# An attention kernel on one core: TensorE's order taken from a written list, some products split into column tiles, the eps sums on another engine

## The chip, the cores and the metric

The kernel runs on one core of a Trainium2 chip. The core has TensorE (PE in the profile; PEld is its weight load), VectorE (DVE), ScalarE (ACT), GpSimd (POOL) and SyncE (SP), which issues nearly all DMAs here. The metric is the device time of one execution in microseconds. Three runs of the kernel before gave 334.11, 334.47 and 336.25 us; the median, 334.47, is the time to beat.

## The reference

Two independent attention layers over 2,048 tokens of width 640, with 32 heads of 20; their outputs stand side by side.

```python
# A: four segments of 512 tokens, with a memory M, z carried from one to the next
for s in range(N):
    qs, ks, vs = (q[:, :, s].copy(), k[:, :, s].copy(), v[:, :, s].copy())
    logits = jnp.einsum('bhqd,bhkd->bhqk', qs, ks) * scale + mask      # causal within the segment
    p = _softmax(logits, axis=-1)
    a_dot = jnp.einsum('bhqk,bhkd->bhqd', p, vs)
    pq = phi(qs)                                                       # t + 1 if t > 0 else exp(t)
    num = jnp.einsum('bhld,bhde->bhle', pq, M)
    den = jnp.einsum('bhld,bhd->bhl', pq, z)[..., None] + 1e-06
    a_mem = num / den
    o = g * a_mem + (1.0 - g) * a_dot
    outs.append(o)
    pk = phi(ks)
    M = M + jnp.einsum('bhld,bhle->bhde', pk, vs)
    z = z + jnp.einsum('bhld->bhd', pk)
return o @ wo
# B: the same projections from one wqkv; scores of a window of 256 tokens, softmax, p @ v, @ wo
```

## The kernel before, in words

The work is cut into eight chunks of 512 tokens, numbered n = 0 to 7: A and B take turns (even n is A, odd n is B). For each chunk TensorE makes the projections q and k (five pieces of 128 columns, each five products of 512 columns; `qk_job`), v (two halves of four tiles, each five products of 320 columns; `v_job`), the scores, the value sums, for A from the second segment on the memory products (`mem`) and the update of the memory (`dm_job`), and at last the output products (`final_job`, `last_job`). All whole-array products pass through `wide` (L870).

Scores come in 153 batches (`score_batch`, L758). A batch fills two of three score buffers in PSUM; ScalarE takes the exponential of each (L774), GpSimd cuts the triangles (L813) or VectorE multiplies the small end squares (L791). A batch can start only when ScalarE has emptied the first buffer of the batch before. What TensorE does between two batches I call a visit: visit i lies between batch i-1 and batch i, counted from 0. When all batches of a group of four heads are done, the value sum of that group follows (`av`, L827; for the last chunk `av_tile`, L848): four column tiles of 32 work side by side, one head each. VectorE turns the result (L883) and takes the reciprocal of the denominators (L908), GpSimd multiplies (L918). For a memory product of an A chunk, VectorE first adds eps to the denominators (L903) and then takes the reciprocal (L906); GpSimd multiplies into a buffer u and VectorE adds it to the output (L931).

All other results of TensorE go through two PSUM banks, m0 and m1, which VectorE empties: q and k (L501), v (L677, L682), outputs (L1027).

The array has three modes here: whole (128 rows by 128 columns), four row tiles of 20 rows for scores, four column tiles of 32 columns for value sums.

The o of a finished chunk is stored to DRAM by SyncE (L949) and read back transposed (L968, DMA_TRANSPOSE) as the weights of the output products. The transposed tile of chunk n takes a buffer that chunk n-2 used, so its transpose is issued after the last output product of chunk n-2. The last chunk is stored and transposed in four tiles; the fourth is turned on TensorE instead (L1049, L1061).

The order of the instructions on every engine is fixed when the program is built, by a planner. Class `Flow` keeps a clock for each engine with costs written in the code; `body` walks its loop: a score batch if its buffer is free, otherwise a value sum or memory product whose inputs are there by those clocks (one queue, `pend`), otherwise a step of the first job in the list that can go. Evictions and small vector work are put on their engines by `at`, `when_idle` and `blocked` by the same clocks. `room` holds back batches of small squares and value sums when TensorE got more than 160 matmuls within 3 us. On the chip each engine follows its own list in order and waits on semaphores.

## Time and profile before

| | |
|---|---|
| median of three runs | 334.47 us |
| the profiled execution | 334.4 us |
| its span, first to last instruction | 331.6 us |
| granted clock of TensorE | 1.000 |
| TensorE busy | 315.6 us (95%), 6583 matmuls recorded |
| ScalarE busy | 302.4 us (91%) |
| VectorE busy | 264.2 us (80%) |
| GpSimd busy | 256.3 us (77%) |
| DMA | 47.36 MB, mean 143 GB/s |
| first exponential starts, last ends | 9.1 us, 318.3 us |

Busy times are unions of what the profiler recorded; matmuls and exponentials overlap with their successors, so the distance from one start to the next tells more than a duration. Times in timelines are microseconds from the first instruction; a row is start, length, engine, line, operation, tiles, shape and count, and in brackets the idle time ahead of it with what ended it. "Issue" is a wait that no semaphore of the profile explains. A few per cent of the matmul records are missing.

### The profile page before, as it was taken

How to read it: one execution, taken by the hardware profiler on the slowest of the kernel's cores; microseconds unless marked ns; L12 is line 12 of the kernel's file. 1: busy time of each engine (PE TensorE's matmuls, PEld its weight loads, DVE VectorE, ACT ScalarE, POOL GpSimd, SP SyncE). 2: the span in 40 equal slices, each digit the busy share in tenths (PEclk: the TensorE clock that was granted, in tenths of full speed). 3: DMA queues.
4: the chain of work that ended last, by engine and by line, in shares of the span. 5: the costliest groups of instructions: out<-in, count | busy, mean ns of one | idle time of the engine just before them, and what ended most of it. 6: DMA issues, size and time to landing. Idle time of an engine off the chain costs nothing.

```text
span 331.6 us, 15794 instructions
## 1 busy us (share of the span) xinstructions
PE 315.6 (95%) x6583; PEld 174.4 (53%) x6619; DVE 264.2 (80%) x556; ACT 302.4 (91%) x333; POOL 256.3 (77%) x648
## 2 busy tenths in 40 slices
PE   8999999999999999989999999999999999999896
PEld 3444546455444455546644545455654545666564
DVE  6777767798978899989868898888667889876654
ACT  1979999999999999999999999989999999999841
POOL 8366689998659799975867879996875969977750
DMA  6975746566596852335699145044555154769852
GB/s 198 396 253 152 173 135 125 136 175 176 132 226 132 165 155 63 67 86 122 183 208 181 42 94 156 3 104 80 148 140 114 21 150 122 166 142 187 178 127 100
DMA packets 76260, 47.36 MB, mean 143 GB/s; under 512 B 48381, under 2 KB 73181, under 8 KB 76189
## 3 DMA queue, kind: packets, MB, share of 16 engines
q1 hardware_dynamic: 75469, 45.71, 56.7%
q8 instruction: 51, 0.84, 1.1%
q10 hardware_dynamic: 720, 0.66, 0.7%
q14 instruction: 20, 0.16, 0.2%
HBM read 17.62 MB, written 16.96 MB: 104 GB/s over the span
## 4 chain that ended last, share of the span: by engine, by line
PE 57%; DVE 15%; ACT 10%; issue 7%; POOL 6%; DMA 3%; SPq 1%; ACTq 0%; DVEq 0%; POOLq 0%
PE m L870 36%; PE sc L758 11%; ACT pt L774 10%; PE m L827 6%; POOL pt L813 4%; DVE pt L791 4%; PE m L848 2%; DVE tt L883 2%; POOL u L918 2%; DVE pq L542 2%; DVE kA L501 2%; DVE vA L677 1%; DMA xT<-in_A_x_dram 1%; DVE pq L536 1%; DVE ot L1027 1%
## 5 line engine op out<-in xcount | busy, mean ns | idle before, releaser
L774 ACT ACTIVATE pt<-sc 128x1024 bf16<-128x1024 f32 (+2 forms) x306 | 285.0, 1012 | 10.7 <-PE sc L758 8.6
L813 POOL TENSOR_SCALAR_AFFINE_SELECT pt<-pt 128x128 bf16<-128x128 bf16 (+1 forms) x512 | 177.1, 374 | 60.4 <-ACT pt L774 57.4
L883 DVE STREAM_TRANSPOSE tt<-m 128x512 f32<-128x512 f32 x88 | 61.4, 711 | 20.0 <-PE m L827 9.1
L918 POOL TENSOR_TENSOR o<-tt,rr 128x320 bf16<-128x320 f32 x64 | 47.8, 747 | 4.1 <-DVE rr L908 4.0
L870 PEld LDWEIGHTS <-xT 128*128 128x128 bf16 x350 | 32.0, 97 | 24.2 <-issue 12.3
L758 PE MATMUL sc<-qB,kB 20*64 20x64 bf16 (+2 forms) x1728 | 38.6, 218 | 1.4 <-issue 0.8
L791 DVE TENSOR_TENSOR pt<-pt,ends 128x1024 bf16<-128x1024 bf16 (+2 forms) x50 | 36.3, 740 | 0.0
L758 PEld LDWEIGHTS <-kB 20*64 20x64 bf16 (+1 forms) x1728 | 21.7, 98 | 23.3 <-issue 22.0
L758 PE MATMUL sc<-qA,kA 20*64 20x64 bf16 (+4 forms) x1024 | 33.1, 237 | 0.5
L1027 DVE CAST ot<-m 128x320 bf16<-128x320 f32 x56 | 26.9, 485 | 7.4 <-PE m L870 7.1
L870 PEld LDWEIGHTS <-oT 128*128 128x128 bf16 x280 | 24.7, 98 | 11.4 <-issue 1.1
L870 PE MATMUL m<-wBv,xT 128*128 128x320 bf16 x160 | 27.0, 299 | 2.4 <-DVE tt L883 2.3
L870 PE MATMUL m<-wv_A,xT 128*128 128x320 bf16 x160 | 26.0, 299 | 2.0 <-DVE vA L677 1.9
L870 PE MATMUL m<-xT,wBq 128*128 128x512 bf16 x96 | 26.4, 381 | 0.4 <-issue 0.2
L870 PE MATMUL m<-xT,wq_A 128*128 128x512 bf16 x88 | 25.0, 381 | 1.8 <-DVE vA L677 0.8
L870 PE MATMUL m<-xT,wk_A 128*128 128x512 bf16 x96 | 25.6, 388 | 1.1 <-DVE qA L501 0.7
L870 PE MATMUL m<-xT,wBk 128*128 128x512 bf16 x84 | 24.8, 381 | 0.8
L758 PEld LDWEIGHTS <-kA 20*128 20x128 bf16 (+1 forms) x1024 | 13.5, 97 | 20.6 <-issue 19.6
L827 PE MATMUL m<-pt,vA 128*32 128x192 bf16 (+3 forms) x512 | 23.6, 275 | 0.0
L870 PE MATMUL m<-wo_A,oT 128*128 128x320 bf16 x140 | 22.7, 300 | 0.2
L501 DVE CAST kB<-m 128x512 bf16<-128x512 f32 x20 | 13.8, 691 | 9.4 <-PE m L870 9.4
L870 PE MATMUL m<-wo_B,oT 128*128 128x320 bf16 x120 | 19.4, 300 | 0.3 <-DVE ot L1027 0.3
(112 smaller groups left out, 405.3 us busy)
## 6 DMA issues: line engine op xcount, KB each, us to landing
out_dram<-ot SPq DMA_DIRECT2D x29, 160.0 KB
scr_o<-o SPq DMA_DIRECT2D x28, 160.0 KB
xT<-in_B_x_dram SPq DMA_DIRECT2D x8, 288.0 KB
xT<-in_A_x_dram SPq DMA_DIRECT2D x8, 256.0 KB
scr_pk<-e SPq DMA_DIRECT2D x15, 128.0 KB
vS<-vA SPq DMA_DIRECT2D x16, 87.0 KB
vL<-vB SPq DMA_DIRECT2D x8, 174.0 KB
scr_kA<-kA SPq DMA_DIRECT2D x16, 60.0 KB
```

The source lines that it names most:

```text
L501: nc.vector.tensor_copy(out=dst[:, m, at:at + L], in_=ps[:, :])
L542: nc.vector.tensor_tensor(out=r if len(box) == 1 else e, in0=r, in1=e, op=ALU.min)
L758: nc.tensor.matmul(ps[j // 2][h0:h1, j % 2, c0:c0 + nq], lhsT=k[rows, g, k0:k0 + h1 - h0], rhs=q[rows, g, q0:q0 + nq], start=True, stop=Tr ...
L774: nc.scalar.activation(out=pt[:, :, lo:hi], in_=ps[i][:, :, lo:hi], func=ACT.Exp, scale=self.scale)
L791: nc.vector.tensor_tensor(out=blk, in0=blk, in1=self.ends[:, c0, :].unsqueeze(1).unsqueeze(1) .to_broadcast([P, 2, n // SH, SH]), op=ALU.mult)
L813: nc.gpsimd.affine_select(out=blk, in_=blk, pattern=pat, compare_op=ALU.is_ge, fill=self.zero, base=base, channel_multiplier=mul)
L827: nc.tensor.matmul(O[HD * j:HD * j + HD, q0:q0 + nq], lhsT=v[:, at_head(h):at_head(h) + HD], rhs=pts[j // 2][:, j % 2, c0:c0 + nq], start= ...
L848: nc.tensor.matmul(O[HD * j:HD * j + HD, o0:o0 + nq], lhsT=v[:, at_head(h):at_head(h) + HD], rhs=pts[j // 2][:, j % 2, c0:c0 + nq], start= ...
L870: self.nc.tensor.matmul(ps[:, 0:n], lhsT=lhsT, rhs=rhs, start=start, stop=stop)
L883: self.nc.vector.transpose(out=tt[:], in_=O[:, :])
L918: nc.gpsimd.tensor_tensor(out=to[:] if add_to else to, in0=a, in1=b, op=ALU.mult)
L1027: nc.vector.tensor_copy(out=ot[:, 320 * hf:320 * hf + 320], in_=ps[:, 0:320])
```

## The change

TensorE's order is now a written list, `PLAN`. An entry is a unit and a count: S or s is the next score batch, A the next value sum, M the next memory product, and a letter with chunk and piece one product (k, q, v, o), one piece of the memory update (d) or one step of the end (z0). `k70*7` is seven products of k of chunk 7. The loop only takes what stands first in the list; the planner's clocks say when, and still place everything on the other engines. Memory products have a queue of their own, `memq`, and wait in the planner for the group's value sum.

In a visit that starts with a capital S and has a value sum in it, `wide` issues each product as four products of 32 columns each into the four column tiles. There are 42 such visits, the last one visit 117; the list's last part has small s only, or no value sum.

The eps sum goes from VectorE to GpSimd. The planner's model changes: the fetch of instruction blocks takes the place of `room`, VectorE and GpSimd hold each other up on some operations, and several costs are lower. No DMA and no other computation is added or removed.

```diff
@@ -26,11 +26,13 @@
 EPS = 1e-6
 NPT = 10
 AT = 0
-FETCH = 160
-FETCH_NS = 3000
+BLOCK = 256
+BLOCK0 = 170
+BLOCK_NS = 3900.0
 BACK = 800.0
 NTT = 4
 QPOOL = 750.0
+EPS_NS = 170.0
 GAP = 48
 GATE = 9800.0
 NM = 20
@@ -53,6 +55,32 @@
 LANES = 8
 AHEAD = 100.0
 LEAD = 500.0
+HOLD = 1
+SPARE = 150.0
+COL_NS = 3.0
+PLAN = (
+    "k00*5 q00*5 k01*4 S k01 q01*5 S v00*16 S v00*4 k02 S k02*4 k03*5 q02*3 S q02*2 q03*5 k04*5 "
+    "A S A q04*5 v01 s v01*9 s k10*5 S v01*10 S q10*2 A S q10*3 q11*3 S q11*2 q12*5 A s k11*5 "
+    "k12*2 S k12 A k12*2 S v10*9 S v10*10 S v10 A k13*2 s k13*3 q13*4 S q13 A s k14*5 q14*2 S "
+    "q14*2 A q14 S d2*5 v11*4 S v11*8 S v11*3 A v11 S v11*4 d2*2 S q20*4 A s q20*5 s q20*6 "
+    "k20*6 S k20*4 A s k20*5 v20*5 S v20*3 A v20 s v20 q23*5 v20 s v20*8 S v20 q23*5 A s v21*5 "
+    "k23*3 S k23*2 A s o00*5 k23*5 v21*5 S o00*5 v21*5 S A v21*5 s q30*5 k30*2 S k30*3 A s "
+    "k30*6 S k30*4 q30 S q30*4 A s M q30*5 v30*2 s v30*3 A S M v30*10 s A M s v30*5 q33*4 S q33 "
+    "A s M k33*5 q33 s q33*4 k33*3 S k33*2 A s M v31*8 S v31*2 A M S v31*10 S A M S d4*5 q40*3 "
+    "S q40*2 d4*2 A s M k40*5 s q40*10 S v40*5 k40*5 A S k40*5 v40*5 S v40*2 A v40*2 S v40*6 "
+    "q43*3 S q43*7 S k43*10 A S o00*5 A s o10*10 s o00*5 o10*5 S o00*10 v41*4 S v41 o10*5 A "
+    "o00*2 s o00*3 v41*5 S A o00*5 s v41*8 s v41*2 o10*7 S o10*3 A o10*3 s o10*2 q50*5 S A "
+    "k50*3 s k50*2 k53*5 s q50*5 k50*2 s k50*3 A S k50*2 M k50*3 s A M S v50*5 q50*5 s A M S "
+    "v50*10 S v50*5 A s M q53*6 s q53*4 k53*2 S k53*3 A S M v51*9 S v51 A M S v51*10 S A M S "
+    "q60*5 d6*5 s d6*2 A S k60*2 M k60*3 q60*5 s k60*6 S k60*4 q60*5 A S q63*5 v60*5 S A v60*5 "
+    "s q63*5 v60*2 S v60*3 k63*5 S v60*5 A k63 S k63*4 o10*5 S o20*3 A s o20*7 s v61*10 S v61*5 "
+    "A v61*5 S o30*5 o20*5 S o20*5 A o20 S o20*4 o30*4 s o30 o20*10 S A o20*4 S o20 k70*7 S k70 "
+    "A k70*2 S k70*5 v70*3 S v70*2 q70*4 s q70 A s M q70*6 s q70*4 A s k73*5 s v70*5 A s M "
+    "v70*7 s v70*3 A M s q73*2 M q73*3 s k73*5 q73*2 s q73*3 A s M o30*5 s v71*5 A s M o30*5 "
+    "v71 s v71*4 A M s v71*10 s A M s o30*10 s o40*5 o30*5 s o30*5 A s o40*10 s o40*10 A o40*5 "
+    "s o40*5 o50*3 s o50*2 o40*5 o50*2 s o50*3 A s o50*10 s A o50*2 s o50*9 s o50*9 s A o60*5 s "
+    "o60*5 o70*5 A o70 s o70*4 o60*5 s o60*5 o71*4 s o71*6 o60*2 s o60*6 A o60*8 A o60*4 o72*2 "
+    "z0*4 ")
 
 def at_head(h):
     return VS * h + 12 * (h // 16)
@@ -97,23 +127,26 @@
                     self.slow[m] = had < (0.355 if self.slow.get(m - 1, True) else 0.31)
         return not self.slow[k]
 
-    def room(self, n):
 ...
     def on_pe(self, mode, ns, cols, ready=0.0, n=1):
-        self.issued.append((max(self.pe, ready), n))
-        return self.on_pe_(mode, ns, cols, ready)
+        self.count += 1
+        if mode != self.mode:
+            self.pe += 97.0
+            self.mode = mode
+        t = max(self.pe, ready)
+        self.on_pe_(mode, ns, cols, ready)
+        first, self.sent = self.sent, self.sent + 2 * n
+        at = (first - BLOCK0) // BLOCK + 1
+        while BLOCK * at + BLOCK0 <= self.sent:
+            x = t + (self.pe - t) * (BLOCK * at + BLOCK0 - first) / (2.0 * n)
+            wait = self.block - x
+            if wait > 0.0:
+                self.starved += wait
+                self.pe += wait
+                t += wait
+                x += wait
+            self.block = x + BLOCK_NS
+            at += 1
+        return self.pe + 215.0
 
     def on_pe_(self, mode, ns, cols, ready=0.0):
         if mode != self.mode:
@@ -867,8 +923,18 @@
 
     def wide(self, ps, lhsT, rhs, n, start, stop):
 
-        self.nc.tensor.matmul(ps[:, 0:n], lhsT=lhsT, rhs=rhs, start=start, stop=stop)
-        self.f.on_pe("full", mm_ns(n), n)
+        f = self.f
+        if self.by_tiles:
+            for j in range(4):
+                s = slice(HD * j, HD * j + HD)
+                self.nc.tensor.matmul(ps[s, 0:n], lhsT=lhsT[:, s], rhs=rhs, start=start,
+                                      stop=stop, tile_position=(0, HD * j),
+                                      skip_group_check=True)
+            f.on_pe("col", n / 2.4 + COL_NS, n, 0.0, 4)
+        else:
+            self.nc.tensor.matmul(ps[:, 0:n], lhsT=lhsT, rhs=rhs, start=start, stop=stop,
+                                  skip_group_check=True)
+            f.on_pe("full", mm_ns(n), n)
         self.f.left = 0 if stop else self.KT - 1 if start else self.f.left - 1
 
     def turn(self, O, bi):
@@ -898,15 +964,18 @@
             a = a.rearrange("p (g b) d -> p g b d", g=4)
             b = b.rearrange("p (g b) d -> p g b d", g=4)
 
-        def s1():
+        def s0():
+            nc.gpsimd.tensor_single_scalar(out=rr[:], in_=tv[:, :, DH], scalar=EPS, op=ALU.add)
+            t = f.on_pool(EPS_NS, t0)
+            f.when_idle(t, lambda: s1(t))
+
+        def s1(te=None):
             if add_to:
-                nc.vector.tensor_single_scalar(out=rr[:], in_=tv[:, :, DH], scalar=EPS,
-                                               op=ALU.add)
-                f.on_dve(100.0, t0)
                 nc.vector.reciprocal(out=rr[:], in_=rr[:])
+                t1 = f.on_dve(276.0, te)
             else:
                 nc.vector.reciprocal(out=rr[:], in_=tv[:, :, DH])
-            t1 = f.on_dve(276.0, t0)
+                t1 = f.on_dve(276.0, t0)
             f.at(t1 - 100.0, lambda: s2(t1))
 
         def s2(t1):
@@ -929,14 +998,17 @@
                     return
                 self.adds.remove(add)
                 nc.vector.tensor_tensor(out=dst, in0=dst, in1=to[:], op=ALU.add)
-                t3 = f.on_dve(300.0, t2)
+                t3 = f.on_dve(210.0, t2, True)
                 self.done_with(uslot, t3)
                 if last:
                     last(t3)
             self.adds.append(add)
             f.when_idle(t2, add)
 
-        f.when_idle(t0, s1)
+        if add_to:
+            f.at(t0 - 100.0, s0)
+        else:
+            f.when_idle(t0, s1)
 
     def final(self, n, o, scr, wo, out2d, r0, col, t0, t1, t):
 
@@ -1338,11 +1410,26 @@
         started = -1
         i = 0
         late = [(19500.0, self.zero_end), (45000.0, self.consts_e), (60000.0, self.consts_one)]
+        plan = PLAN.split()
+        plan = [x.split("*")[0] for x in plan for _ in range(int((x + "*1").split("*")[1]))]
+        visits, tiles = [False], False
+        for x in plan:
+            if x in "Ss":
+                visits.append(False)
+                tiles = x == "S"
+            elif x == "A" and tiles:
+                visits[-1] = True
+        plan.reverse()
+        over = set()
         while True:
             f.flush()
             times = []
             self.all_scored = i == len(bs)
-            if i < len(bs):
+            while plan and plan[-1] in over:
+                plan.pop()
+            want = plan[-1] if plan else None
+            self.by_tiles = bool(plan) and visits[i]
+            if i < len(bs) and want in (None, "S", "s"):
                 n, ent, ms, complete = bs[i]
                 kind, c = chunks[n]
                 if self.ring("pt", NPT) is not None:
@@ -1351,8 +1438,10 @@
                         for w in "kq":
                             need.append(self.done.get((n, w, e[0])))
                     if None not in need:
-                        t = max(need + [f.room(4 * len(ent)) if ent[0][1][0] in "lust" else 0.0])
-                        if t <= f.pe and not self.may_wait():
+                        t = max(need)
+                        if t <= f.pe and (want or not self.may_wait()):
+                            if want:
+                                plan.pop()
                             if n != started:
                                 started = n
                                 self.seed(n + 1)
@@ -1368,40 +1457,59 @@
                             for g in complete:
                                 pend.append((n, g, "tile" if n == NC - 1 else "av"))
                                 if kind == "A" and c > 0:
-                                    pend.append((n, g, "mem"))
+                                    memq.append((n, g))
                             i += 1
                             if i == len(bs) or bs[i][0] != n:
                                 self.mark(f.seen, n, "scored")
                             continue
                         times.append(t)
             soon = times[-1] if times else None
-            if pend:
+            if pend and want in (None, "A"):
                 n, g, what = pend[0]
                 kind, c = chunks[n]
                 if what == "tile":
                     ps_ = [p for x in range(4) for p in parts[(n, g[1] + x)]
                            if p[1] // P == g[0]]
                     need = [whole(p[6] for p in ps_), self.done.get((n, "v", g[1]))]
-                elif what == "av":
+                else:
                     ps_ = parts[(n, g)]
                     need = [whole(p[6] for p in ps_), self.done.get((n, "v", g))]
-                else:
-                    need = [self.done.get(("dm", c - 1)),
-                            self.done.get((n, "pq", g) if g < KT else (n, "pq2"))]
-                if None not in need and not (f.open and 0 < f.left <= 3):
-                    t = max(need + [min(f.bank_free), f.room(
-                        4 * len(ps_)) if what != "mem" else 0.0])
+                if None not in need and (want or not (f.open and 0 < f.left <= 3)):
+                    t = max(need + [min(f.bank_free)])
                     wait = (f.mode == "full" and soon is not None and len(pend) < 3
                             and soon < f.pe + 2200.0 and self.more(f.pe))
-                    if t <= f.pe and not wait:
+                    if t <= f.pe and (want or not wait):
+                        if want:
+                            plan.pop()
                         pend.pop(0)
                         self.one_group(n, kind, c, g, what, parts, left, o_t, groups_done,
+                                       scro, wo, out2d)
+                        continue
+                    times.append(t)
+            if memq and want in (None, "M"):
+                n, g = memq[0]
+                kind, c = chunks[n]
+                need = [self.done.get(("dm", c - 1)),
+                        self.done.get((n, "pq", g) if g < KT else (n, "pq2")),
+                        self.done.get((n, "add", g))]
+                if None not in need and (want or not (f.open and 0 < f.left <= 3)):
+                    t = max(need[:2] + [min(f.bank_free)])
+                    after = f.pe + mm_ns(L) + (97.0 if f.mode != "full" else 0.0)
+                    wait = (len(memq) < HOLD and max(f.bank_free) > after + SPARE
+                            and self.more(f.pe))
+                    if t <= f.pe and (want or not wait):
+                        if want:
+                            plan.pop()
+                        memq.pop(0)
+                        self.one_group(n, kind, c, g, "mem", parts, left, o_t, groups_done,
                                        scro, wo, out2d)
                         continue
                     times.append(t)
             hit = None
             for x, jb in enumerate(self.jobs + self.fins):
                 if f.open and not jb[0] is self.opener:
+                    continue
+                if want and jb[2] != want and (jb[2][0] != "d" or jb[1] in ("bank", 0.0)):
                     continue
                 t = self.need_time(jb[1])
                 if t is None:
@@ -1420,6 +1529,10 @@
                     jb[1] = next(jb[0])
                 except StopIteration:
                     (self.jobs if jb in self.jobs else self.fins).remove(jb)
+                    over.add(jb[2])
+                if f.count != was:
+                    if want:
+                        plan.pop()
                 while late and f.pe > late[0][0]:
                     late.pop(0)[1]()
                 continue
```

Left out are the changed planner costs (`on_dve`, `on_pool` and their callers), the labels given to jobs, and the mark that the value sum of a group is normalised.

More of the change, by code (lines that the diff above doesn't have):

```diff
@@ L87, in __init__ @@
         self.slow = {}
-        self.issued = []
+        self.sent, self.block, self.starved = 0, 0.0, 0.0
+        self.dve_at, self.pool_at = [], []
+        self.count = 0
     def full_rate(self, t):
@@ L98, in full_rate @@
         return not self.slow[k]
-    def room(self, n):
-        while self.issued and self.issued[0][0] <= self.pe - FETCH_NS:
-            self.issued.pop(0)
-        have = n + sum(k for _, k in self.issued)
-        t = self.pe
-        for t0, k in self.issued:
-            if have <= FETCH:
-                break
-            have -= k
-            t = t0 + FETCH_NS
-        return t
-    def on_pe(self, mode, ns, cols, ready=0.0, n=1):
-        self.issued.append((max(self.pe, ready), n))
-        return self.on_pe_(mode, ns, cols, ready)
+    def on_pe(self, mode, ns, cols, ready=0.0, n=1):
+        self.count += 1
[17 more added lines that the diff above has]
+        return self.pe + 215.0
     def on_pe_(self, mode, ns, cols, ready=0.0):
@@ L137, in on_act, with held, on_dve @@
         return self.act + 181.0
-    def on_dve(self, ns, ready=0.0):
-        self.dve = max(self.dve, ready) + ns
+    def held(self, t, by):
+        for a, b in by:
+            if a <= t < b - 65.0:
+                return b - 65.0
+        return t
+    def on_dve(self, ns, ready=0.0, shared=False):
+        t = max(self.dve, ready)
+        if shared:
+            t = self.held(t, self.pool_at)
+            self.dve_at = self.dve_at[-7:] + [(t, t + ns)]
+            for x, (a, b) in enumerate(self.pool_at):
+                if t < a < t + ns - 65.0:
+                    late = t + ns - 65.0 - a
+                    self.pool_at[x:] = [(p + late, q + late) for p, q in self.pool_at[x:]]
+                    self.pool += late
+                    break
+        self.dve = t + ns
         return self.dve + 138.0
     def on_pool(self, ns, ready=0.0):
-        self.pool = max(self.pool, ready) + ns
+        t = self.held(max(self.pool, ready), self.dve_at)
+        self.pool_at = self.pool_at[-11:] + [(t, t + ns)]
+        self.pool = t + ns
         return self.pool + 98.0
@@ L1163, in batches, with job @@
         return out
-    def job(self, gen):
-        return [gen, next(gen)]
+    def job(self, gen, label):
+        return [gen, next(gen), label]
     def may_wait(self):
@@ L1222, in seed @@
                     need = [tx, gate] + ([self.known("wB" + what, some[0])] if first else [])
-                    add(self.qk_job(n, what, some, w, dst, need, self.scr[what + kind][c], phi))
+                    add(self.qk_job(n, what, some, w, dst, need, self.scr[what + kind][c], phi),
+                        "%s%d%d" % (what, n, some[0]))
                 if first and some[0] == AT:
-                    add(self.late_v())
+                    add(self.late_v(), "v01")
             if first:
                 v[3] = v[3] + [self.known("wBv", half)]
-            add(self.v_job(n, half, *v))
+            add(self.v_job(n, half, *v), "v%d%d" % (n, half))
     def body(self, xA, A_wq, A_wk, A_wv, A_wo, A_beta, xB, B_wqkv, B_wo, out2d):
@@ L1318, in first @@
                                       self.known(0, "x", KT - 1 if m else 0)],
-                                     scr[what + "A"][0], phi)))
+                                     scr[what + "A"][0], phi),
+                         "%s0%d" % (what, m)))
         for m in range(KT):
@@ L1415, in body @@
                 jb = (self.jobs + self.fins)[hit]
+                was = f.count
                 if jb[1] == "bank":
@@ L1438, in body @@
             f.pe = max(f.pe + 1.0, min(times))
-        assert i == len(bs) and not pend and not self.jobs and not self.fins
+        assert i == len(bs) and not pend and not memq and not self.jobs and not self.fins
     def used_pt(self, left, i, g):
```

28 lines of the change are left out of this document (14 added, 14 removed).

## The prediction

> **What bounds the kernel.** I read the page first, then the timeline of TensorE, then the groups with their shapes kept apart, the waits, and the tail in every engine's timeline. The execution that was profiled took 334.4 us, its span 331.6, so 2.8 us lie around the span; the median of the three runs is 334.47, and I work with 334.4. A difference under about 1% (3.3 us) could not be told from no change.
>
> The page's totals, the 40 slices of TensorE and ScalarE, and the instruction queue:
> ```profile
> PE 315.6 (95%) x6583; PEld 174.4 (53%) x6619; DVE 264.2 (80%) x556; ACT 302.4 (91%) x333; POOL 256.3 (77%) x648
> ...
> PE   8999999999999999989999999999999999999896
> ...
> ACT  1979999999999999999999999989999999999841
> ...
> q8 instruction: 51, 0.84, 1.1%
> ```
> Two engines are full from slice 3 to slice 38, in step with each other: a score batch may not start before ScalarE has emptied the buffers of the one before. Busy times overlap with themselves, so I take durations from starts. TensorE's timeline near the end, and a value sum of chunk A:
> ```profile
> 96.60 0.59 PE L827 MATMUL m<-pt,vA 128*32 128x448 bf16 x12
> 97.02 0.29 PE L827 MATMUL m<-pt,vS 128*32 128x64 bf16 x16
> 97.14 0.20 PE L827 MATMUL m<-pt,vA 128*32 128x64 bf16 x4
> ...
> 314.02 0.39 PE L758 MATMUL sc<-qB,kB 20*128 20x128 bf16 x13 [0.84 <-issue]
> 314.35 1.53 PE L870 MATMUL m<-wo_A,oT 128*128 128x320 bf16 x10
> 315.81 0.40 PE L758 MATMUL sc<-qB,kB 20*128 20x128 bf16 x16
> 316.14 0.30 PE L848 MATMUL m<-pt,vB 128*32 128x128 bf16 x8
> ...
> 320.15 2.21 PE L870 MATMUL sc<-wo_A,oT 128*128 128x320 bf16 x15
> 322.20 0.84 PE L870 MATMUL m<-wo_B,xT 128*128 128x320 bf16 x5
> ```
> Fifteen products of 320 columns take 322.20 - 320.15 = 2.05 us, 0.137 each. Ten of them followed by scores take 315.81 - 314.35 = 1.46: ten products (1.36) and 0.10 for the change of mode (whole array, rows in four, columns in four). Counted along the timeline there are 382 changes of mode: 37 us. With 0.137 for 320 columns, 0.216 for 512 (the median distance of two starts), 0.23 for scores of 512 columns, 0.55 for a batch of the small squares and 0.57 to 0.70 for a value sum, TensorE's work is 269 us, with the changes 306. It runs from 0.8 to 328.5, so it stands idle 21 us, 3 of them before the first scores.
>
> ScalarE:
> ```profile
> 314.49 3.77 ACT L774 ACTIVATE pt<-sc 128x1024 bf16<-128x1024 f32 x4 [0.95 <-PE sc L758]
> ```
> Four exponentials in 3.77 us, the last ending 1.03 after its start: 0.913 from start to start. 284 of these, 20 narrower ones at about 0.70 and 18 of phi at 0.95 or 0.55 come to some 288 us, between 9.1 and 318.3: 21 us of slack here too. So neither engine alone is the bound; what counts is how evenly the order spreads TensorE's work over the 153 visits between score batches, and what is left after the last.
>
> **The change, part by part.**
>
> *Changes of mode: -4.3.* Walking the list gives 392 changes if every product used the whole array. In 42 visits the products are split into four column tiles, which takes away 54: 338 remain, 44 fewer than 382, at 0.097. The split costs no array time by the rows above: the twelve matmuls of 448, 320 and 192 columns are three groups of four tiles over 960 columns and take 0.42 us, 0.140 per 320, against 0.137 for a whole product. Weight loads do not show either: 16 matmuls over 64 columns with their 16 loads take 97.14 - 97.02 = 0.12 us, 0.03 for four. The Trainium skill (TensorEngine Tiling (Array Packing), Restrictions and Gotchas) says that column tiling gives up the fast weight load, which speaks against the split. If four loads then stood in line at the 97 ns that the trace gives one, a product of 320 columns would take 0.39 instead of 0.14; the 0.03 above says that they do not.
>
> *Work moved ahead of the last score batch: nothing in the sum of TensorE, +0.6 in balance.* The list leaves 28 output products after the last scores (o60 18, o72 10), where the timeline of before has 60: 32 x 0.137 = 4.4 us leave the tail and enter the visits. The changes of mode saved there just pay for them: visits 1 to 152 hold 287.6 us of TensorE in both orders, ScalarE 287. Taking the larger of the two engines in stretches of eight visits gives 293.1 before, 293.9 after; in stretches of four 295.2 and 297.6, since a few visits of the list are heavy (140: fifteen output products and a value sum, 3.4 us against 1.8 of exponentials). Other visits differ little: 62 of the 64 value sums stand at the same visit. Bounds 0 and +2.4; I take +0.6, nearer to eight, as the exponentials of phi can slide into heavy visits.
>
> *Eps on GpSimd: -2.0.* Groups by shape, then waits (total, times, longest):
> ```profile
> L903 DVE TENSOR_SCALAR rr<-tt 128x16 f32<-128x16 f32 x24 | 8.9, 371 | 0.0
> ...
> L906 DVE RECIPROCAL rr<-rr 128x16 f32<-128x16 f32 x24 | 6.1, 253 | 0.8
> ...
> L651 POOL TENSOR_TENSOR MZ<-mz,bm 128x36 bf16<-128x36 f32 x3 | 1.6, 517 | 0.0
> ...
> PE m L870 <- DVE tt L883: 2.3, 12, 0.2
> ...
> PEld L827 <- DVE rr L906: 2.0, 6, 0.4
> ```
> VectorE loses 24 x 0.37 = 8.9 us, all in the three stages with memory products. The minimum of L903 is 0.15, its median 0.26, its maximum 1.01, so much of this is waiting, not work. What of it reaches TensorE: 2.0 us of value sums that waited for the reciprocal, and the 2.3 us of products behind transposes. Both gone would be -4.3, neither 0; I take the first, -2.0. GpSimd gains 24 sums. The nearest rows are L651 (0.52 mean, 36 elements) and the 0.15 of the cheapest L903: 3.6 to 12 us in stages where it is busy 80% (26.3 of 33.0 us from 91 to 124). I count nothing, because a mask has some two visits until its value sum. Two waits are added: GpSimd's sum waits for VectorE's transpose, with masks and multiplications queued behind it, and VectorE's reciprocal waits for the sum, with evictions behind it. If that cover fails, 24 x 0.1 to 0.2 us reach TensorE, +2.4 to +4.8.
>
> *The tail: +0.7 and +0.8.* SyncE's transposes and a copy of VectorE, from the timeline:
> ```profile
> 306.14 3.90 SPq L968 DMA_TRANSPOSE oT<-scr_o  x1
> ...
> 318.59 1.21 SPq L968 DMA_TRANSPOSE xT<-scr_o  x1
> ...
> 323.54 0.68 DVE L1053 CAST pq<-sc 128x512 bf16<-128x512 f32 x1
> ```
> Before, TensorE never stops after the last scores: output products fill every wait. The list ends with o72 and z0. After z0's first four products the copy (0.68) must be done before the last two halves, and nothing but z0's 16 small matmuls lies beside it: about +0.7, bounds 0 and 1.5. And o72 needs the third transposed tile. Before, the value sum of visit 150 ended near 310.0 and that tile landed at 321.4, used at 322.2: 12.2 us. The list puts the sum in visit 149 and o72 some 10 us of TensorE later. SyncE then waited on other stores, so part of the 12 is queue: +0.8, bounds 0 and 2.8.
>
> *Instruction supply: 0.* Splitting 190 products adds 6 instructions each, 1,140 on 13,202: 56 packets on q8 instead of 51 (259 instructions per packet now). By pure TensorE work, before has 6 stretches of 256 instructions shorter than 3.9 us (the closest packets of q8 start 3.5 to 3.9 us apart), short by 4.8 us together; after has 8, short by 8.3. Most shortfalls vanish since ScalarE holds the pace, which is the cover; the stall of 0.84 at 314.02 is one that showed. Uncovered: +3.5.
>
> *The rest: 0.* Separate queue for memory products, labels, the planner's new costs: they set the order on VectorE, GpSimd and SyncE, no instruction more. The DMAs are the same in number; stores and transposes of the outputs move up by three or four visits on SyncE.
>
> Sum: -4.3 + 0.6 - 2.0 + 0.7 + 0.8 = -4.2: 334.4 - 4.2 = **330.2 us**.
>
> **Rivals.**
>
> *Landings eat the gain: 333.5.* The order is rigid. o30 ends in visit 138 and o50 starts in visit 141: some 7 us, where before o30's end (294.0) to the tile's landing (301.1, after the transpose issued at 296.39) and first safe use took 7.5. The same with o60 after o40 (some 9.5 us against 7.9). Half a microsecond at o50, the full 2.8 at o72 instead of 0.8 and 0.5 elsewhere give +3.0 to +3.3. For it: such waits hide in no other work of a fixed order. Against: two of the three have slack.
>
> *Instruction supply decides, slower: 337.0.* Place: visits 102 to 103, 145 to 146, 64 to 66, 87 to 89, where tiled products, scores and a value sum stand together (200 instructions in one visit against some 125 before). If ScalarE's pace does not cover the shortfalls, the 8.3 us show, of which before already pays about 1.5: +6.8, to 337.0. Five stalls of 0.84 cancel the gain; from there it is slower. Against: the densest visits stand next to thin ones, and packets come ahead of need.
>
> *Split products are dearer: from 341.* If the loads did not hide in part, at 0.06 more for each of 190 products: +11. The value sums' rows speak against it. The loss of the fast weight load in the Trainium skill (same page and section) would be its cause.
>
> **Chances.** Forecast 0.66, own range 325.5 to 333 (0.56 of it below 331.1); landings 0.20; supply 0.11; split products 0.03. Best corner: -4.3 - 4.3 and no waits at the end, 325.8; two of ten left out, the range is 325.5 to 335.5. Faster by over 1% 0.56, within 1% 0.10 + 0.20 + 0.03 = 0.33, slower 0.08 + 0.03 = 0.11.
>
> **What would show it.** Groups of 32-column products on L870's successor in steps of 0.137 and 0.216; some 338 changes of mode; L903 on POOL near 0.2 to 0.5; last scores about 2 to 3 us earlier than 315.8 and a tail of about 13 us instead of 15.8; q8 with 56 packets and no more "issue" gaps on scores. The forecast is wrong if TensorE waits on transposed tiles at o50, o60 or o72, if 0.8 us gaps on "issue" multiply, or if the middle is more even than my stretches say.

## The result, and the profile after

| | before | after |
|---|---|---|
| median | 334.12 us (22 runs) | 332.59 us (22 runs) |
| ratio | | 0.9952, 95% interval 0.9935 to 0.997 |
| profiled execution, its span | 334.4, 331.6 us | 332.5, 330.7 us |
| first scores start | 8.7 | 8.8 |
| first to last scores | 307.1 | 309.1 |
| last scores to the end of the span | 15.8 | 12.8 |

The change gains 1.6 us; I forecast 4.2. The time lies in the range. The ratios here and below leave out runs that took over 1.5% longer than the fastest of their kernel: of the changed kernel's 22 these are two, of 337.6 and 338.1 us. Two later measurements of the same kernel (e9 and e16) gave ratios of 0.9976 (0.9948 to 1.0005) and 0.9969 (0.9939 to 1.0), so 0.8 to 1.6 us is what it is worth.

The page of the changed kernel: totals, the 40 slices of TensorE and ScalarE, and the instruction queue.
```profile
PE 316.4 (96%) x7195; PEld 176.2 (53%) x7195; DVE 255.8 (77%) x533; ACT 299.6 (91%) x333; POOL 265.4 (80%) x672
...
PE   7999999998999999999999999999999999999984
...
ACT  1979999998999998989999999899999999979962
...
q8 instruction: 56, 0.92, 1.2%
```
As before, two engines are full from slice 3 to slice 38, but ScalarE has a dip (7) in slice 36, from 289 to 298 us. The 56 packets are there.

Products split into column tiles, in TensorE's timeline:
```profile
211.94 1.05 PE L930 MATMUL m<-xT,wk_A 128*32 128x512 bf16 x16
212.81 1.25 PE L930 MATMUL m<-xT,wq_A 128*32 128x512 bf16 x20
```
Sixteen matmuls, four products of 512 columns, take 212.81 - 211.94 = 0.87 us: 0.217 each, as a whole product does. The same count of changes of mode as for before gives 338.

The sum of eps on its new engine, and the reciprocal behind it (groups of the page):
```profile
L968 POOL TENSOR_SCALAR rr<-tt 128x16 f32<-128x16 f32 x24 | 7.4, 309 | 2.7 <-DVE tt L949 0.5 <-DVE rr L977 0.3 <-POOL pt L869 0.2
L974 DVE RECIPROCAL rr<-rr 128x16 f32<-128x16 f32 x24 | 5.5, 232 | 0.7 <-POOL rr L968 0.6
```

Who waits for whom (total, times, longest), after, and below it the one row of before that it is to be read against:
```profile
ACT pt L830 <- PE sc L814: 12.9, 23, 1.9
...
PE m L935 <- DVE tt L949: 1.3, 6, 0.3
...
PEld L883 <- DVE rr L974: 1.2, 4, 0.4
```
```profile
ACT pt L774 <- PE sc L758: 8.6, 20, 1.5
```
The two rows that I wanted to shrink did: TensorE behind the transposes 2.3 to 1.3, value sums behind the reciprocal 2.0 to 1.2. But **ScalarE waits for scores 12.9 us instead of 8.6**, and the longest wait is new. It is visit 140, which the list gives fifteen output products and a value sum (L904, not shown) between two score batches:
```profile
290.35 0.40 PE L814 MATMUL sc<-qB,kB 20*128 20x128 bf16 x16
...
290.69 1.53 PE L935 MATMUL m<-wo_A,oT 128*128 128x320 bf16 x10
...
293.01 0.85 PE L935 MATMUL m<-wo_A,oT 128*128 128x320 bf16 x5
...
293.80 0.93 PE L814 MATMUL sc<-qB,kB 20*64 20x64 bf16 x64
...
294.79 4.69 ACT L830 ACTIVATE pt<-sc 128x1024 bf16<-128x1024 f32 x5 [1.95 <-PE sc L814]
```
From scores to scores TensorE needs 293.80 - 290.35 = 3.45 us. ScalarE has two exponentials, 1.83 us, to do in that time, and stands still for 1.95.

The end, TensorE's timeline:
```profile
313.98 0.85 PE L935 MATMUL m<-wo_A,oT 128*128 128x320 bf16 x5
...
315.68 0.72 PE L935 MATMUL m<-wo_B,xT 128*128 128x320 bf16 x4 [0.84 <-DMA xT<-scr_o]
...
317.92 0.40 PE L814 MATMUL sc<-qB,kB 20*128 20x128 bf16 x16
...
324.60 0.30 PE L1133 MATMUL sc<-one,o 128*32 128x32 bf16 x16
...
325.46 0.72 PE L935 MATMUL m<-wk_A,pq 128*128 128x320 bf16 x4 [0.56 <-DVE pq L1125]
```
The last scores start 2.1 us later than before, and the tail behind them is 3.0 us shorter. The products of o71 wait 0.84 us for their transposed tile, those of z0 0.56 for the copy.

### The profile page after: what moved, and what is told of

It reads as the page before. It is cut to its first block, busy times and chain, and to the rows that moved or that the text cites. A ratio compares the mean times of both kernels' runs of the same rounds, so it can differ in the third digit from the quotient of the medians.

```text
span 330.7 us, 16968 instructions
## 1 busy us (share of the span) xinstructions
PE 316.4 (96%) x7195; PEld 176.2 (53%) x7195; DVE 255.8 (77%) x533; ACT 299.6 (91%) x333; POOL 265.4 (80%) x672
## 4 chain that ended last, share of the span: by engine, by line
PE 36%; DVE 5%; ACT 3%; DMA 2%; POOL 2%; issue 1%; SPq 1%; ACTq 0%; DVEq 0%
PE m L935 19%; PE sc L814 7%; PE m L883 5%; ACT pt L830 3%; PE m L930 2%; DVE tt L949 2%; PE m L904 1%; DMA xT<-scr_o 1%; DVE pt L847 1%; DMA scr_o<-o 1%; POOL pt L869 1%; DVE kA L557 1%; POOL o L987 1%; DVE ot L1099 0%; PE m L686 0%
## 5 line engine op out<-in xcount | busy, mean ns | idle before, releaser
L830 ACT ACTIVATE pt<-sc 128x1024 bf16<-128x1024 f32 (+2 forms) x306 | 282.9, 1026 | 15.1 <-PE sc L814 12.9
L949 DVE STREAM_TRANSPOSE tt<-m 128x512 f32<-128x512 f32 x88 | 61.2, 709 | 24.7 <-PE m L883 15.9
L935 PEld LDWEIGHTS <-xT 128*128 128x128 bf16 x296 | 26.7, 97 | 18.4 <-issue 6.1
L935 PEld LDWEIGHTS <-oT 128*128 128x128 bf16 x244 | 21.5, 97 | 12.5 <-issue 3.3
L935 PE MATMUL m<-wBv,xT 128*128 128x320 bf16 x147 | 24.2, 299 | 0.9 <-DVE tt L949 0.4
L935 PE MATMUL m<-xT,wBq 128*128 128x512 bf16 x82 | 21.4, 380 | 0.3 <-DVE tt L949 0.3
L935 PE MATMUL m<-xT,wBk 128*128 128x512 bf16 x81 | 20.7, 381 | 0.0
L935 PE MATMUL m<-wv_A,xT 128*128 128x320 bf16 x119 | 20.0, 300 | 0.2 <-DVE vA L733 0.2
L738 DVE CAST vB<-m 128x320 bf16<-128x320 f32 x32 | 15.6, 488 | 5.4 <-PE m L935 3.1
L557 DVE CAST qB<-m 128x512 bf16<-128x512 f32 x20 | 13.8, 688 | 6.7 <-PE m L930 3.4
L935 PE MATMUL m<-xT,wk_A 128*128 128x512 bf16 x69 | 17.7, 379 | 1.2 <-DMA xT<-in_A_x_dram 1.1
```

Of the source, the lines that this page charges most:

```text
L557: nc.vector.tensor_copy(out=dst[:, m, at:at + L], in_=ps[:, :])
L738: nc.vector.tensor_copy(out=dst, in_=src)
L830: nc.scalar.activation(out=pt[:, :, lo:hi], in_=ps[i][:, :, lo:hi], func=ACT.Exp, scale=self.scale)
L935: self.nc.tensor.matmul(ps[:, 0:n], lhsT=lhsT, rhs=rhs, start=start, stop=stop, skip_group_check=True)
L949: self.nc.vector.transpose(out=tt[:], in_=O[:, :])
```

## The experiments

Ratios are to the kernel before on the same chip; e1 to e16 name the runs.

**The parts, one taken back at a time.** Whole products only (e2: `self.by_tiles = False` in the loop), the eps sum back on VectorE (e3: `nc.vector.tensor_single_scalar` in `s0`), and the list up to visit 116 followed by the old order, with 30 output products moved up (e4).

> The changed kernel with every product over the whole array, same list. Adds 54 changes of mode at 0.097 us, takes 1,140 instructions away from TensorE. Theory 1 (the split is worth its changes of mode where TensorE is behind): 332.6 plus 2 to 5, so 334.5 to 337.5, q8 back to 51 or 52 packets. Theory 2 (the split costs more than it saves, by instruction supply or dearer products): 332.6 or less.

> The changed kernel with the eps sums back on VectorE (same list, same split; the planner counts 100 ns on VectorE for one). Prediction's step (eps on GpSimd worth 2 us): 334.6. Theory 1 (it is worth nothing, since what waited there was off the path): 332.2 to 333.0. Theory 2 (the sum on GpSimd holds up masks and costs time): 331 or less.

> The changed kernel's list up to visit 116, then the order of before for the remaining visits, with its output products moved up by the 30 that the list has done more by then. Same work. Theory 1 (the list's last part loses to heavy visit 140 and to the wait for the transposed tile at o71, about 2 us together, which an even rhythm of 10 and 5 products does not have): 331 to 332. Theory 2 (the last part of the list is where the gain was made): 333.5 to 335.

Measured: 1.0053 (1.0027 to 1.0079), 1.0004 (0.9979 to 1.0029) and 1.0014 (0.9984 to 1.0044). Against the three measurements of the changed kernel, the split is worth 2.6 to 3.4 us, eps on GpSimd 0.9 to 1.7, the last part of the list 1.3 to 2.1. Only the split is clear of all three measurements; the intervals of the other two overlap with those of e9 and e16, so that they help is likely and not shown. The split takes away 54 changes, 5.2 us of TensorE, and half to two thirds of it arrive.

**The old order under the new planner.** The order of TensorE before, written as a list, whole products only (e1; the start of the list):

```diff
-    "k00*5 q00*5 k01*4 S k01 q01*5 S v00*16 S ...
+    "k00*5 q00*5 k01*4 s k01 q01*5 v00*5 s v00*13 s ...
```

> The changed kernel with TensorE's order of before written out as its list (all small s, so no split products); eps sums on GpSimd, separate queue of memory products and the planner's new clocks stay. The kernel before takes 334.1 us, the changed one 332.6. Theory 1 (the list and the split give all of the gain, the rest is worth nothing): 334 to 335, within 0.3% of before. Theory 2 (my prediction's step: eps on GpSimd gives 2 us by itself): about 332. Theory 3 (eps on GpSimd and the new placement on VectorE, GpSimd and SyncE cost time, which the list has to earn back first): 336 or more.

It came out slower than the kernel before: 1.0118 (1.009 to 1.0146). I suspected the planner's new costs, which order VectorE and GpSimd, and took them back, once in the changed kernel (e5) and once in this one (e6, there without the model of the instruction blocks too); in a third kernel (e7) this one has eps alone taken back. Parts of the edit of e5:

```diff
-        if shared:
+        if False:
...
-        t = self.held(max(self.pool, ready), self.dve_at)
+        t = max(self.pool, ready)
...
-                f.on_dve(235.0, t, True)
+                f.on_dve(300.0, t)
```

> The changed kernel with its list, its split products and the eps sums on GpSimd, but the planner's clocks of VectorE and GpSimd as they were before (no waits for each other's port, the old costs of the four VectorE operations), so that VectorE and GpSimd take their work in an order of the old kind. Theory A (the new clocks' placement is what costs the 3.9 us that the old order lost): the list keeps its gain and that cost goes, about 329 us, ratio 0.985 (0.980 to 0.990). Theory B (eps sums on GpSimd cost it, where the old order leaves no cover for them): nothing changes, 332.5, ratio 0.995. Theory C (no part by itself: a rigid order meets a few late operations by chance, wherever they fall): between 331 and 335.

> The order of TensorE of the kernel before, frozen as a list, whole products only, eps sums on GpSimd, with the planner's old clocks for VectorE and GpSimd and no model of the instruction blocks. Theory A: the 3.9 us of the old order under the new clocks go, 334 or, with the 2 us of the eps sums, 332: ratio 0.994 to 1.000. Theory B: 338, ratio 1.012. Theory C: about 336, ratio 1.005.

> The order of TensorE of the kernel before, frozen as a list, under the new clocks, with the eps sums back on VectorE. Theory A: still slow, 338 or up to 2 us more, ratio 1.012 to 1.018. Theory B: 334, ratio 1.000. Theory C: about 336, ratio 1.005.

Measured: 1.0037 (1.0019 to 1.0054), 1.012 (1.0086 to 1.0154), 1.0081 (1.0055 to 1.0106). **Theory A falls**: the old costs make nothing better in the old order and cost the new list 2 to 2.8 us. Of theory B a part may hold: eps on GpSimd seems to cost the old order 1.2 us, though the intervals overlap. Most of the rest lies in the tail and is a fault of my copy: it lets o71's products fall into the score buffers, and their eviction by ScalarE comes last. This row is at the end of the old order's span of 337.0, where before has none:
```profile
332.58 1.29 ACT L1079 CAST ot<-sc 128x640 bf16<-128x640 f32 x2 [0.47 <-ACT oe L1153]
```
The tails of these kernels are 17.8 to 18.2 us against 15.8. So they do not measure the placement cleanly. Ahead of the tail, from first to last scores, their traces take longer than the one of before by 3.2 us (e1) and 1.8 (e6) with eps on GpSimd, and by 0.5 (e7) with eps on VectorE. That speaks for theory B, from one trace each.

**How long is a stretch that evens out?** The forecast summed the larger of the two engines over stretches of eight visits. Here (e10) six visits of the changed list get five products more, and the next visit five fewer; three of the six:

```diff
-v50*10 S v50*5 A s
+v50*15 S A s
...
-o20*4 o30*4 s o30 o20*10 S
+o20*4 o30*5 o20*4 s o20*6 S
...
-o50*9 s o50*9 s
+o50*14 s o50*4 s
```

> The changed kernel with five products of 320 columns (0.69 us) moved one visit ahead in six places (visits 87, 108, 113, 123, 133, 146), nothing else: the same instructions, the same changes of mode but for one or two, six more heavy visits, each followed by a light one. If what a visit has beyond ScalarE's 1.82 us is lost in that visit (the larger of the two engines summed visit by visit rises by 3.5 us), it takes 335 to 336, ratio 1.002 to 1.006, with ScalarE waiting 0.4 to 0.7 for scores at each place. If the buffers carry it over two visits, +0.9: 333.4, ratio 0.998. If only stretches of eight visits count, as the prediction's +0.6 took it, nothing: 332.5, ratio 0.995.

Measured: 335.72 us, ratio 1.0071 (1.0042 to 1.01), 2.9 us over the changed kernel on the same chip (e9). At the six visits ScalarE now waits 0.47, 0.23, 0.40, 0.25, 1.18 and 0.44 us, 2.97 together; in the trace of the changed kernel it waits at none of them. (In the 1.18, at visit 133, are 0.33 us in which TensorE itself waited for VectorE.) The sum of all its waits over 0.1 us from first to last scores, 15.2 there and 18.0 here, tells less: in the traces of e9 and e16, the changed kernel again, it is 17.2 and 15.9. Visits 87 and 113 in ScalarE's timeline:
```profile
188.60 20.87 ACT L829 ACTIVATE pt<-sc 128x1024 bf16<-128x1024 f32 x22 [0.47 <-PE sc L813]
...
242.97 18.81 ACT L829 ACTIVATE pt<-sc 128x1024 bf16<-128x1024 f32 x20 [0.40 <-PE sc L813]
```
Visit by visit the sum rises by 3.5, over two visits by 0.9, over eight by nothing. 2.9 is nearest to visit by visit: most of what a visit has too much is lost there.

**Evening the list out.** Visits 98 to 102 (e11), and visits 139 to 152 in two ways (e12, and e8, which also has o71 later). The start of e12's edit, then e11's:

```diff
-o40*10 s o40*10 A o40*5 s o40*5 o50*3 s o50*2 o40*5 o50*2 s o50*3 A s
+o40*10 s A o40*5 s o40*10 s o40*10 s o50*5 A s
...
-k60*2 M k60*3 q60*5 s k60*6 S k60*4 q60*5 A S q63*5 v60*5 S A v60*5 s
+k60*2 M k60*3 s q60*5 k60*6 S k60*4 A S q60*5 q63*5 S A v60*10 s
```

> The changed kernel with two edits of its list near the end: five output products of o40 leave the visit that held fifteen of them, with the products behind it moved on, and o71's ten products stand some six products later, with o60's in their place, so that the transposed tile has landed. Nothing else. If the heavy visit and the late tile cost what the trace shows beside them (0.84 us of waiting at o71, a delay of 1.5 us of the scores behind the heavy visit), it takes about 331.3, ratio 0.991. If ScalarE's pace decides there and the delay is made up anyway, 332.5, ratio 0.995.

> The changed kernel with visits 98 to 102 evened: the five products of q60 that stood in visit 98 and the five in visit 100 move one visit on, v60's five behind them. Visit by visit the sum falls by 0.9, over two visits by 0.6, over eight by 0. ScalarE's waits of 1.26 and 0.42 us there should go. Lost visit by visit: 331.2 to 331.6, ratio 0.991 to 0.993. Made up within eight visits: 332.5, ratio 0.995. If something else holds those visits (a landing, VectorE): 332.5 or more, with the wait moved on by a visit.

> The changed kernel with visits 139 to 152 evened: no visit has more than ten output products, or five and a value sum; the last scores then have two products more behind them (0.27 us), and o71's products stand later, so that its tile has landed. Visit by visit the sum falls by 1.6, over two visits by 1.3, over eight by 0.6; ScalarE's waits of 1.95 (visit 140), 0.80 (149) and 0.81 (151) should go. Lost visit by visit: 330 to 331, ratio 0.987 to 0.991. Over eight: 332.2, ratio 0.994. If a block of instructions comes late behind o60's transposing transfer, as it did in the smoother end (2.24 us there), 333 to 334, ratio 0.997 to 1.000, with the stall called issue in TensorE's row.

Measured: 1.0027 (1.0003 to 1.0051), 1.0037 (1.0006 to 1.0068), 0.9991 (0.997 to 1.0012). None is faster than the changed kernel. (Part of that is the clock, below: the runs of e8 and e11 at a mean granted clock of 0.997 and above have medians of 333.4 and 334.1 us.) In e12 the wait at visit 140 falls from 1.95 to 1.11, the one at visit 151 goes, and new ones come at 141 (0.73) and 145 (1.46); in e11 the wait of 1.26 at visit 98 comes back as 1.45 at visit 101. There the moved products wait for VectorE to empty a bank, in TensorE's timeline:
```profile
214.41 2.32 PE L934 MATMUL m<-xT,wq_A 128*128 128x512 bf16 x10 [0.74 <-DVE kA L556]
```
In e8 and e12 it is the stall on issue that the expectation of e12 names. TensorE's timelines, e8 and then e12:
```profile
305.43 0.57 PE L813 MATMUL sc<-qB,kB 20*64 20x64 bf16 x43 [2.24 <-issue]
```
```profile
304.75 0.51 PE L812 MATMUL sc<-qB,kB 20*64 20x64 bf16 x41 [1.17 <-issue]
```
A batch stops in the middle, on no semaphore; I put it down to a block of instructions that is not there yet. Its packet started at 303.0 in e8, 7.8 us after the one before it, and at 302.0 in e12, 6.3 after; both at the end of o60's transposing transfer (299.5 to 303.2 and 299.9 to 302.8). In the changed kernel a packet starts at 300.2, just ahead of that transfer (300.6). So I moved the transfer in e12 behind o70's (e14):

```diff
-            f.blocked.append((tl - 200.0, room, lambda t_: turn(tl)))
+            f.blocked.append((tl - 200.0 + (3500.0 if n == 6 else 0.0), room, lambda t_: turn(tl)))
```

> The kernel with visits 139 to 152 evened, and SyncE issues o60's transposing transfer behind the next store and behind o70's transfer, some 4 us later; it is still ahead of its first product. If a block of instructions can't come while a transposing transfer runs: the packet of the instruction queue that came at 302.0, at the end of that transfer, comes near 299.5, the stall of 1.17 us on issue in the middle of a score batch near 304 goes, and the time falls by about 1.2, ratio 0.994 to 0.997. If the instructions there are simply too many for the queue: packets and stall stay where they are, 333.8, ratio 0.999.

The packet comes at 301.7, not at 299.5, but in a trace that runs 1.2 us later there: it starts 4.5 us after its predecessor instead of 6.3, ahead of the transfer (302.1). The stall of 1.17 is gone, and ScalarE's wait at visit 145 falls from 1.46 to 0.18. From visit 132 to the last scores e14 loses 1.8 us on the kernel before, e12 3.2. The total does not show it (0.9989, 0.996 to 1.0018): this trace had lost 1.2 us more before visit 132, and totals of two chips differ by as much.

**o71's tile.** The second edit of e8 alone (e13):

```diff
-s o60*5 o71*4 s o71*6 o60*2 s o60*6 A
+s o60*9 s o60 o71*5 o60*2 s o60*3 o71*5 A
```

> The changed kernel with o71's ten products some six products later in the list and o60's in their place, nothing else, so that the transposed tile has landed when they come. If the 0.84 us that TensorE waits for that tile is on the path that sets the end: 331.8, ratio 0.993 to 0.994. If the score batches behind it are paced by ScalarE and the blocks of instructions anyway: as the changed kernel, 332.6, ratio 0.995 to 0.998.

Measured: 0.9954 (0.9921 to 0.9986), beside the changed kernel's 0.9969 (0.9939 to 1.0) on the same chip. The wait is gone from the timeline. Whether its 0.84 us reach the end can't be told from these times. The traces say that most of it does: from visit 132 to the last scores e13 takes 0.7 us more than the kernel before, the changed kernel in its three traces 1.6 to 1.8, and e13's tail is only 0.1 longer. No version here is clearly faster than the changed kernel.

**The clock.** The mean granted clock of a run was never below 0.997 in 118 runs of the kernel before, and was in 12 of 46 of the changed kernel. To tell the split from the order, e2 once more (e15):

> The changed kernel with whole products only, once more, for the granted clock: with the new list and split products about one run in three has a mean clock below 0.997 (3 of 12 in the last look at the changed kernel), the kernel before has none in over 80. If the split products draw the lower clock: no run of this kernel below 0.997. If the new order does: 3 or 4 of 12. Time as before, 335.5, ratio 1.003 to 1.006.

None of 12 without the split (22 with e2), against 3 of 12 for the changed kernel beside it; the time, 1.005 (1.0027 to 1.0072), repeats e2. In five places inside the work, in the traces of e3, e8, e9 and e11, the clock drops to one half for 3.41 us, and each time TensorE has stood still just before, for 1.67 to 3.30 us. Windows of e8 (length, busy time of PE, PEld, DVE, ACT, POOL, then PEclk, DMA share, GB/s):
```profile
302.10:305.50 3.40, 1.16 (x75) 0.71 (x67) 0.97 (x2) 1.67 (x2) 3.39 (x8) 1.00 1.08 217
305.50:308.90 3.40, 3.40 (x68) 1.90 (x68) 1.11 (x3) 1.94 (x2) 0.00 (x0) 0.51 0.44 104
```
That is the stall on issue of 2.24 us. In the first repeat of the changed kernel a value sum waits 2.18 us near 81 us, and the same follows:
```profile
78.50:81.90 3.40, 1.22 (x29) 0.51 (x32) 0.81 (x4) 2.89 (x4) 0.91 (x4) 1.00 0.34 77
81.90:85.30 3.40, 3.29 (x107) 2.30 (x100) 3.17 (x7) 1.80 (x2) 3.02 (x6) 0.50 0.28 77
```
So a stall of about 2 us can be paid nearly twice. It need not be: in e10 TensorE is busy only 1.47 us between 78.7 and 82.1 us, and the clock stays whole. The Trainium skill (TensorE: Matmul & The Clock Gate, Part 1: The HAM clock gate) says that an idle window of some 3.4 us halves the clock; the length and the half agree, but here 1.16 or 1.22 us of work in such a window did not prevent it. Runs of the changed kernel at 0.997 and above have medians of 332.3, 332.8 and 332.5, those below reach 338.1.

## Why the prediction was right and wrong

By its own steps:

- **Changes of mode, -4.3: right on TensorE, not in the total.** 382 became 338 in the traces, and split products take a whole product's time. But TensorE ends only 1.5 us earlier (327.0 for 328.5) with 4.3 us less to do: it stands idle 2.8 us more. The rival of dear split products is out. So is the loss that the Trainium skill (TensorEngine Tiling (Array Packing), Restrictions and Gotchas) ties to column tiling, the fast weight load: 0.217 for four tiles shows none.
- **Work moved ahead of the last scores, +0.6 in balance: this step failed.** It took stretches of eight visits as the unit, and the three score buffers do not carry work over that far. From first to last scores the forecast was -1.4 (+0.6, and -2.0 for eps), measured +2.0; the last scores, which I wanted 2 to 3 us earlier (my own sum gives 1.4), start 2.1 later. Counted again from the matmuls in the traces (the old order from e1, which has all of before's products in the same visits and lacks no record), the larger of the two engines rises by some 0.5 to 1.2 us over eight visits, as forecast, by 2 to 4 over two and by 3 to 4.6 visit by visit, depending on which batch is set against which exponentials; that is an estimate. Less the 0.9 to 1.7 of eps, one or two visits give about the +2.0, eight do not. e10 decides between one and two, for visit by visit.

  ScalarE's waits over 0.1 us rise from 9.4 to 15.2, and the long ones stand where the list is heavy: visits 140 (1.95), 98 (1.26), 67 (1.17), 4 (1.09), 149 (0.80). Not all of that is new loss. Over its pace of 0.904 us from start to start, ScalarE loses 23.0 us in the old order and 25.6 in the new one: delays too short to show as a gap of 0.1 fall from 10.5 to 6.1, the others rise from 12.5 to 19.5. The old order lost a little in many visits, the new one much in a few. The reason was in the text that I had before me: a batch takes two of three score buffers, so ScalarE can have little more than one visit in store.

  What is not shown is the way back: e8, e11 and e12 take work out of heavy visits and gain nothing, since late instruction blocks or VectorE took the place of the wait. So e10 shows what an uneven visit costs, and no run shows that an evened list would have brought the 4.2.
- **Eps on GpSimd, -2.0: too much.** 0.9 to 1.7 in the new list, within the noise of two of the three measurements of the changed kernel; in the old order it seems to cost time. The mean is 0.31 us, within 0.2 to 0.5.
- **The tail, +0.7 and +0.8: right in sum, one in the wrong place.** z0 waits 0.56 for the copy. o72 does not wait; o71 does, 0.84, ahead of the last scores. Tail 15.8 to 12.8, forecast about 13.
- **Instruction supply, 0: right for the trace after, wrong as a rule.** It has no gap on issue at the scores and the old one of 0.84 is gone; the trace of e9, the same kernel, has one of 0.8. e8 and e12 show how close it is, and a stall can bring the half clock with it. I had no term for the clock.
- **The rest, 0.** Not settled by the frozen orders; with the new list the new costs help by 2 to 2.8 us (e5), so the list and the costs belong together. I had put them at nothing because they add no instruction; the order that they set counts too.
- Around the span: 1.7 us in the changed kernel's median, 2.0 in that of before, 0.3 that no step spoke of.

Of the rivals, landings had the time nearest to the result (333.5), but by another mechanism: one tile was late, by 0.84, and it was neither o50's nor o72's, on which the rival built. That its time is near is luck.

## What to carry to other kernels

Where two engines hand work to each other through a few buffers, sum the larger of the two over what the buffers hold, not over what looks like a smooth stretch: with three buffers and two used per batch, that was about one visit here. Time saved on one of them counts only where it is the later one. And before evening such a list out, look where its instruction blocks and its transposing transfers fall: a stall of 2 us can cost nearly twice that in the clock.

## What the runs showed of the hardware

In these traces blocks of instructions hardly start while a transposing transfer runs. In the 18 traces of this study 953 packets of the instruction queue start between 20 and 325 us; in the inner part of those transfers (0.6 us after their start to 0.8 before their end) 11 do, where evenly spread ones would be 67, and 97 start in the 1.1 us around their ends, where 41 would. e14 is the one deliberate test of it.

The granted clock is one or one half in these traces. Inside the work the half comes in five spans of 3.41 us, each behind a stretch of that length in which TensorE was busy 0.4 to 1.8 us; others begin in the last 10 us of a kernel and run past its end. Of 158 runs without split products one had a mean below 0.997, of 152 with them 46. Of the five stalls three are on issue in the middle of a score batch (1.67 us in e3, 2.24 in e8, 1.90 in e11), one is a value sum that waits for VectorE (2.18 in e9) and one an output product that waits for its transposed tile (3.30 in e11). All five are in kernels with split products. That the split, with its 1,140 instructions more, brings the stalls on issue fits this; it is not shown.
